# Redrawing the head of a fused linear-attention and squared-ReLU kernel: order of the first steps, place of one bias fetch, and the cut of the first weight block

## The chip, the cores and the metric

The kernel runs on one core of one Trainium2 chip. The metric is the device time of one execution in microseconds, lower is better. Where a profile is read, its times run from the start of the profiled span. Engines are named as the profile names them: PE (TensorE matmul), PEld (its weight load), DVE (VectorE), ACT (ScalarE), POOL (GpSimd) and SP (SyncE); SPq and ACTq are the queues on which SP and ACT issue DMAs.

## The reference, cut to what matters

```python
x = A_x                                   # 1 x 2048 x 448, bf16
xn = layernorm(x)                         # no scale, no shift, eps 1e-5
# A: linear attention, 16 heads of 28
q, k, v = split(xn @ wqkv)                # wqkv 448 x 1344
phi = lambda t: where(t > 0, t + 1, exp(t)) + 1e-6
kv = einsum("hsd,hse->hde", phi(k), v);  z = sum over s of phi(k)
s = (phi(q) @ kv / (phi(q) . z + 1e-6)) @ wo
# B: squared-ReLU block, 448 -> 1792 -> 448
h = relu(xn @ w1 + b1) ** 2
g = silu(h @ w2 + b2)
return x + s * g
```

## The kernel before, in words

The 2048 tokens are 16 tiles of 128 tokens, in 4 groups of 512. The 448 channels are 3 chunks of 128 and a rest of 64; matmuls on the rest use half of PE's rows, and the long streams pair two units on the two halves of the rows. The hidden width of 1792 is 14 chunks of 128.

A `Program` collects operations (`add`) with an engine, the tiles they read and write, and an assumed duration. PE and SP run in the order in which the program adds the operations: that order is written out by hand. The operations of ACT and DVE are ordered by a planner (`schedule`, `one_pass`) that walks through assumed times, assumed landing times of transfers among them; `behind` ties one operation behind another on its engine, `prio` puts it ahead. Every engine then runs its list strictly in order, waiting on semaphores. PSUM has 8 banks, which the planner hands out.

The **head** is what happens until the first long stream of matmuls. Its steps, by the labels used below:

- `load_x`, `load_main`, `load_rest`: DMAs. Tokens 0 and 1 one by one, 2 and 3 together; then k's weights (`wk`: chunks 0 to 2 on SP, the rest channels twice, one for each half of the rows, on ACT); then `w1` in blocks set by `cuts` (`w10`, `w11`, `w12`, `w13`, each with two rests), with the bias `b1r` behind `w10`. `late_loads` then queues the gates' bias `b2b`, the two halves of `w2` and q's weights `wq`.
- `bn`, `ag` (line 497, 498, DVE), `ln`, `rs` (505, 509, ACT), `xn` (527, DVE): layer norm of one tile. `tw` (543 on DVE, 544 on ACT) doubles the rest channels of a pair of tiles.
- `warm` (line 1223): matmuls on a zero tile that keep PE busy.
- `T0` to `T3` (`pe_transpose`, line 604): PE transposes the three full chunks of a tile; `eT` (613 on DVE, 614 on ACT) evicts them to `xT`. `TR0`, `TR2` (`pe_transpose_rests`, 628): the rests of a pair of tiles; `eTR` (638) evicts them.
- `K0.0`, `K1.0` (`k_part`, 803): k of tiles 0 and 1 on the full chunks; `Kr0` (`k_rests`, 818): their rest, with both `wk` rests. `phi` (709, 714, 721) turns them into phi(k).
- `Ha0.0`, `Ha1.0`, `Ha0.2`, `Ha1.2` (`head_part`, 831): hidden chunks 0 and 1 for tiles 0 and 1, then for tiles 2 and 3; `Hr0` (`head_rest`, 847): the rest. `B1`, `b1f` (`bias_cols`, 1238, 1241): transpose of `b1`, which every ReLU (line 766) needs.

Then follows the stream `H0.2` to `H0.13` (line 788): twelve hidden chunks of group 0, four at a time, then the second matmul (`G`, line 1094), k, q and so on, all in one order by hand.

Of the kernel before, what the change touches and what calls it, by code (L numbers as in the profile page):

```python
# [9 lines left out]
P = 128  # L10
S, D, F = 2048, 448, 1792
# [35 lines left out]
class Program:  # L47
# [6 lines left out]
    def add(self, eng, emit, reads=(), writes=(), dur=0.2, alts=(), nbytes=0, mode=None, label="", slow=1.0):  # L54
        op = Op(eng, emit, reads, writes, dur, alts, nbytes, mode, label)
        op.slow, op.behind, op.at = slow, None, None
        for t in op.reads:
            op.raw.add(self.writer[t])
            self.readers.setdefault(t, []).append(op)
        for t in op.writes:  # L60
            w = self.writer.get(t)
            if w is not None and w is not op:
                op.deps.add(w)
            for r in self.readers.get(t, ()):
                if r is not op:
                    op.deps.add(r)
            self.writer[t] = op
            self.readers[t] = [r for r in self.readers.get(t, ()) if r is op]
        op.raw.discard(op)
        op.deps |= op.raw  # L70
        for d in op.deps:
            d.succ.append(op)
        self.ops.append(op)
        return op
# [233 lines left out]
def bass_recurrent_scan__linear_attn_block__dense_activation_squared_relu__prompt_kernel(  # L308
    nc, A_x, A_wqkv, A_wo, B_x, B_w1, B_b1, B_w2, B_b2, out
):  # L310
    with ExitStack() as es:
# [3 lines left out]
        add = pr.add  # L315
# [4 lines left out]
        eps5 = sb("eps5", [P, 1], f32)  # L320
# [5 lines left out]
        x_tok = sb("x_tok", [P, NT, D], bf)  # L326
        xn = sb("xn", [P, NT, 512], bf)
        xT = sb("xT", [P, NT, 4, P], bf)
# [7 lines left out]
        b1r = sb("b1r", [NF, P], bf)  # L336
        b1f = sb("b1f", [P, NF], f32)
        b2b = sb("b2b", [P, D], bf)
        st6 = sb("st6", [P, NT, 6], f32)
# [26 lines left out]
        def ap(src, dims, offset=0):  # L366
            return bass.AP(tensor=src.tensor, offset=src.offset + offset, ap=dims)
# [59 lines left out]
        def dma(eng, dst, src, writes, nbytes, reads=(), dur=0.45, slow=1.0):  # L427
            return add(
                eng, lambda e, _: e.dma_start(dst, src), reads, writes, dur, nbytes=nbytes, label="dma" + str(writes[0]), slow=slow  # L429
            )  # L430
# [11 lines left out]
        def load_rest(eng, w, src, name, lo, hi, off=0, part=None):  # L442
            for i in (0, 1) if part is None else (part,):
                dma(
                    eng, w[64 * i : 64 * i + 64, 3, lo:hi], src[384:448, off + lo : off + hi], [(name, 3 + i)],
                    64 * (hi - lo) * 2, ["actw"] if eng == "act" else (), dur=0.58,
                )

        wn = lambda name: [(name, i) for i in range(5)]
        HA = 2  # L450
        cuts = (0, 4 * P, 6 * P, 10 * P, F)
        add("act", lambda e, _: e.preload_act_table_set("natural_log_exp_and_others"), [], ["actw"], 1.25, label="table").prio = -1e6
        load_x(0, 1, "sp")
        load_x(1, 2, "sp")
# [17 lines left out]
        late_constants()  # L472

        def late_loads():
            dma("sp", b2b[:, :], ap(B_b2, [[0, P], [1, D]]), ["b2b"], P * D * 2)
            for i, at in ((0, 17.9), (1, 20.8)):
                f0 = i * NF // 2
                dma(
                    "sp", w_2[:, f0 : f0 + NF // 2, :], B_w2[P * f0 : P * (f0 + NF // 2)].rearrange("(f p) d -> p f d", p=P),
                    [("w2", i)], F * D,  # L480
                ).at = at
            load_main("sp", w_q, A_wqkv, "wq", 0, D)
            load_rest("sp", w_q, A_wqkv, "wq", 0, D)

        def last_loads():
            load_x(12, 16)
# [6 lines left out]
        def hp(si, k):  # L493
            return None if si > 3 else 5 * si + k - 25

        def ln_stats(si):
            add("dve", lambda e, _: e.bn_stats(st6[:, si, :], x_tok[:, si, :]), [("x", si)], [("st", si)], 0.61, label=f"bn{si}").prio = hp(si, 0)  # L497
            add("dve", lambda e, _: e.bn_aggr(mv[:, si, :], st6[:, si, :]), [("st", si)], [("mv", si)], 0.16, label=f"ag{si}").prio = hp(si, 1) if si > 1 else si - 29

        def ln_rstd(lo, hi):  # L500
            c = slice(lo, hi)
            ts = range(lo, hi)
            add(
                "act",
                lambda e, _: e.activation(out=vep[:, c], in_=mv[:, c, 1], func=AF.Ln, bias=eps5[:, 0:1]),
                [("mv", i) for i in ts] + ["eps5", "actw"], [("vep", i) for i in ts], 0.3, label=f"ln{lo}",
            ).prio = -40 + lo if hi - lo == 1 else None
            add(
                "act", lambda e, _: e.activation(out=rstd[:, c], in_=vep[:, c], func=AF.Exp, scale=-0.5),  # L509
                [("vep", i) for i in ts], [("rstd", i) for i in ts], 0.2, label=f"rs{lo}",  # L510
            ).prio = -40 + lo if hi - lo == 1 else None

        def xn_cols(si, lo, hi):
# [20 lines left out]
        def ln_twin(lo, hi):  # L534
            ts = range(lo, hi)

            def twin(e, eng):
                dst, src = xn[:, lo:hi, 448:512], xn[:, lo:hi, 384:448]
                if lo >= 4 * SWAP:
                    both = xn[:, lo:hi, :].rearrange("p t f -> p (t f)")  # L540
                    dst, src = both[:, 896:1024], both[:, 768:896]
                if eng == "dve":
                    return e.tensor_copy(dst, src)
                return e.activation(out=dst, in_=src, func=AF.Copy)

            add("dve", twin, [("xn", i) for i in ts], [("xd", i) for i in ts], 0.18, alts=[("act", 0.27)], label=f"tw{lo}").prio = hp(lo + 1, 4)

        MM = lambda n: n / 2400 + 0.0025

# [69 lines left out]
                    0.15 + 0.07 * n if eng == "dve" else 0.18 + 0.107 * n, label=f"eT{si}.{lo}",  # L619
                ).prio = -30  # L620

        def pe_transpose_rests(lo):
            b = Buf("T")

            def f(e, _):
                v = ps(b)[:, :].bitcast(bf)
                for i in range(2):
                    last = e.transpose(v[:, i * P : (i + 1) * P], xn[:, lo + i, 384:512], ident[:, :])
                return last

            ts = (lo, lo + 1)
            add("pe", f, [("xd", i) for i in ts] + ["ident"], [b], 0.0558 * 2, mode="128", label=f"TR{lo}")

            def ev(e, eng):
                src = ps(b)[:, 0:P].bitcast(bf).rearrange("p (t k) -> p t k", t=2)
                if eng == "dve":
                    return e.tensor_copy(xT[:, lo : lo + 2, 3, :], src)
                return e.activation(out=xT[:, lo : lo + 2, 3, :], in_=src, func=AF.Copy)

            add("act", ev, [b], [("xT", i) for i in ts], 0.39, label=f"eTR{lo}").prio = -30  # L640

        def pe_transpose_two(lo):
            b = Buf("T")
# [573 lines left out]
        def warm(n, after=(), src=None):  # L1217
            b = Buf("W")

            def f(e, _):  # L1220
                last = None
                for _i in range(n):
                    last = e.matmul(ps(b)[:, 0:P], src or dum[:, 0:P], src or dum[:, 0:P], start=True, stop=True)
                return last

            add("pe", f, ["dum", *after] if src is None else [], [b], n * 0.107, mode="128", label="warm")
# [15 lines left out]

        warm(3, src=one)
        warm(30)
        warm(8, [("mv", 0)])
        pe_transpose(0, ((0, 3, "act"),))
        warm(3)
        pe_transpose(1, ((0, 3, "act"),))
        k_part(0, 0, 3)
        pe_transpose_rests(0)  # L1250
        k_part(1, 0, 3)
        head_part(0, 0)
        pe_transpose(2, ((0, 3, "act"),))
        head_part(0, 1)
        bias_cols()
        pe_transpose(3, ((0, 3, "dve"),))
        pe_transpose_rests(2)
        k_rests(0)
        head_part(2, 0)
        head_part(2, 1)  # L1260
        head_rest(0)

        byname = {op.label: op for op in pr.ops}
        for first, order in (
            (-26, "bn0 ag0 bn1 ag1 xn0 xn1 bn2 ag2 bn3 ag3 xn2 xn3"),
            (-61, "rs1 eT0.0 tw0 eT1.0 ln2 rs2 ln3 rs3 eTR0 eT2.0 b1f"),
        ):
            names = order.split()
            for i, (a, b) in enumerate(zip(names, names[1:])):
                byname[b].behind = byname[a]  # L1270
                byname[b].prio = first + 1 + i
            if first < -26:
                byname[names[0]].prio = first
        landing = {
            ("x", 0): 2.92, ("x", 1): 3.9, ("x", 2): 4.65, ("wk", 0): 5.7, ("wk", 3): 5.7, ("wk", 4): 7.2, ("w10", 0): 6.97,
            ("w10", 3): 7.2, ("w10", 4): 7.4, ("b1r", None): 7.5, ("w11", 0): 8.2, ("w11", 3): 8.4, ("w11", 4): 8.6,
            ("w12", 0): 9.7, ("w12", 3): 9.9, ("w12", 4): 10.1, ("x", 4): 11.3,
        }
        for (name, k), t in landing.items():
            byname["dma" + str((name, k) if k is not None else name)].at = t  # L1280
# [135 lines left out]
```

## Time and profile before

| | us |
|---|---|
| median of 3 runs | 143.53 (143.05 to 143.62) |
| profiled execution, its own time | 143.35 |
| its span | 142.1 |
| busy PE / DVE / ACT | 138.3 / 103.0 / 79.1 |
| first matmul of the stream `H0.2`.. | 10.82 after the start |
| last matmul but the tail's | about 138.3 |

The span leaves 1.25 us of the profiled execution's own time outside. In the rows of the timeline the first number is the start, the second the time from the first start to the last end of a merged row, and `x3` the number of instructions in it; ends of matmuls are modelled, so that the distance between starts, not the duration, gives the pace. A bracket tells how long the engine sat idle before the row and what released it.

### The profile page before, as it was taken

Reading aid. Unit: us, or ns where it says so; the run is one execution under the profiler, and the core shown is the slowest. Engines: PE = TensorE matmul, PEld = TensorE weight load, DVE = VectorE, ACT = ScalarE, POOL = GpSimd, SP = SyncE. Lnnn points to the kernel's source line nnn. Section 1 sums busy time; section 2 is a strip of 40 time slices with the busy share of each in tenths; the row PEclk is TensorE's granted clock in tenths of the full one; section 3 lists DMA queues with packets and bytes.
Section 4 is the critical chain, followed back from the end, with each engine's and each line's share of the span. In section 5 each row is a group of like instructions: output and inputs, shape, how many; then the busy total and the mean of one; then the engine's idle time right before and its main releaser. Section 6 shows DMA issues by size and latency. Waiting matters only on the chain.

```text
span 142.1 us, 3239 instructions
## 1 busy us (share of the span) xinstructions
PE 138.3 (97%) x1299; PEld 71.1 (50%) x1299; DVE 103.0 (72%) x222; ACT 79.1 (56%) x146; POOL 6.3 (4%) x40
## 2 busy tenths in 40 slices
PE   7999999999999999999999999999999999999992
PEld 7854445454444444444544444445547455555472
DVE  2848984899889897789777799786035516874875
ACT  3679797140888727697962757697139430301412
POOL 7900000000000000000000000000000000000000
PEclk9999999999999999999999999999999999999999
DMA  4998997349923000232000000000696000223033
GB/s 96 322 277 241 276 342 160 47 58 283 198 33 55 14 0 0 46 51 46 12 5 0 0 0 5 0 0 19 161 210 152 0 0 24 94 81 102 32 97 97
DMA packets 24220, 12.91 MB, mean 91 GB/s; under 512 B 14354, under 2 KB 23566, under 8 KB 24206
## 3 DMA queue, kind: packets, MB, share of 16 engines
q1 hardware_dynamic: 22414, 11.35, 31.8%
q10 hardware_dynamic: 1792, 1.36, 4.0%
q8 instruction: 10, 0.16, 0.5%
q14 instruction: 4, 0.03, 0.1%
HBM read 9.23 MB, written 1.90 MB: 78 GB/s over the span
## 4 chain that ended last, share of the span: by engine, by line
PE 91%; DMA 4%; DVE 2%; SPq 1%; issue 0%
PE pb L788 29%; PE pb L1094 22%; PE pb L1186 7%; PE pb L889 7%; PE pb L731 7%; PE pb L741 6%; PE pb L1111 4%; DMA w<-in_B_w_dram 4%; PE pb L1151 3%; PE pb L868 1%; SPq L429 1%; PE pb L831 1%; DVE gbuf L1175 1%; PE pb L895 1%; PE pb L1038 1%; PE pb L963 1%
## 5 line engine op out<-in xcount | busy, mean ns | idle before, releaser
L788 PE MATMUL pb<-xT,w 64*128 64x512 bf16 x378 | 43.6, 376 | 0.0
L1094 PE MATMUL pb<-w,r 64*128 64x448 bf16 x336 | 34.6, 349 | 0.0
L766 ACT ACTIVATE r<-pb,b1f 128x512 bf16<-128x512 f32 x40 | 25.7, 686 | 14.2 <-PE pb L788 13.8
L788 PEld LDWEIGHTS pb<-xT,w 64*128 64x128 bf16 x378 | 18.2, 94 | 21.8
L1094 PEld LDWEIGHTS pb<-w,r 64*128 64x128 bf16 x336 | 16.2, 94 | 16.0 <-issue 0.4
L778 ACT ACTIVATE r<-r 128x1024 bf16<-128x1024 bf16 x15 | 15.7, 1062 | 0.3
L763 DVE TENSOR_SCALAR r<-pb,b1f 128x512 bf16<-128x512 f32 x16 | 11.7, 744 | 3.2 <-PE pb L788 3.2
L1206 DVE TENSOR_TENSOR gbuf<-pb,gbuf 128x448 bf16<-128x448 f32 x14 | 8.1, 618 | 6.6 <-PE pb L1186 6.6
L497 DVE BATCH_NORM_STATS2 st<-x_tok 128x6 f32<-128x448 bf16 x16 | 9.6, 613 | 4.4 <-DMA x_tok<-in_A_x_dram 4.4
L731 PE MATMUL pb<-w_k,xT 64*128 64x448 bf16 x98 | 11.5, 349 | 0.0
L741 PE MATMUL pb<-xT,w_q 64*128 64x512 bf16 x84 | 11.0, 376 | 0.0
L1134 ACT ACTIVATE gbuf<-gbuf 128x448 bf16<-128x448 bf16 x14 | 7.0, 570 | 6.5 <-DVE gbuf L1084 5.9
L1186 PE MATMUL pb<-w_k,pqT 64*128 64x448 bf16 x96 | 10.5, 349 | 0.0
L1084 DVE TENSOR_TENSOR gbuf<-pb,b2b 128x448 bf16<-128x448 f32 x14 | 8.0, 614 | 3.4 <-PE pb L1094 2.0
L721 DVE SCALAR_TENSOR_TENSOR pk<-pb,pk 128x448 bf16<-128x448 f32 x16 | 9.6, 619 | 0.2
L889 PE MATMUL pb<-pk,xn 128*128 128x448 bf16 x48 | 9.6, 353 | 0.0
L709 ACT ACTIVATE pk<-pb 128x448 bf16<-128x448 f32 x16 | 7.8, 543 | 3.1 <-PE pb L731 2.5
L1002 DVE TENSOR_TENSOR pqT<-pqT,xT 128x2048 bf16<-128x2048 bf16 x3 | 3.7, 1222 | 8.0 <-DMA xT<-scr 8.0
L527 DVE TENSOR_SCALAR xn<-x_tok,mv,rstd 128x448 bf16<-128x448 bf16 x16 | 7.4, 499 | 1.6 <-ACT rstd L509 1.6
L777 DVE TENSOR_TENSOR r<-r 128x1024 bf16<-128x1024 bf16 x13 | 8.5, 682 | 0.1
L925 DVE TENSOR_TENSOR zacc<-zacc,pk 128x448 f32<-128x448 f32 x13 | 8.0, 617 | 0.1
L709 ACT ACTIVATE pqT<-pb 128x512 bf16<-128x512 f32 x12 | 6.5, 597 | 2.1 <-PE pb L741 2.1
(100 smaller groups left out, 134.1 us busy)
## 6 DMA issues: line engine op xcount, KB each, us to landing
w<-in_B_w_dram SPq DMA_DIRECT2D x2, 784.0 KB, 8.5
out_dram<-gbuf SPq DMA_DIRECT2D x14, 112.0 KB, 1.7
w<-in_B_w_dram SPq DMA_DIRECT2D x3, 384.0 KB, 4.9
xT<-gbuf SPq DMA_DIRECT2D x32, 32.0 KB, 2.0
x_tok<-in_A_x_dram SPq DMA_DIRECT2D x2, 448.0 KB, 5.7
x_tok<-in_A_x_dram SPq DMA_DIRECT2D x3, 224.0 KB, 3.1
xT<-scr SPq DMA_DIRECT2D x6, 112.0 KB
xT<-scr ACTq DMA_DIRECT2D x5, 112.0 KB
```

The source lines that it names most:

```text
L497: add("dve", lambda e, _: e.bn_stats(st6[:, si, :], x_tok[:, si, :]), [("x", si)], [("st", si)], 0.61, label=f"bn{si}").prio = hp(si, 0)
L709: "act", lambda e, _: e.activation(out=slot, in_=ps(buf)[0:rows, 0:n], func=AF.Exp), [buf, "actw"],
L721: lambda e, _: e.scalar_tensor_tensor(out=slot, in0=ps(buf)[0:rows, 0:n], scalar=1.0 + 1e-6, in1=slot, op0=ALU.add, op1=ALU.max),
L731: return e.matmul(ps(b)[:, 0:D], x_tile(rows, si, c), w_k[rows, c, :], start=start, stop=stop)
L741: return e.matmul(ps(b)[:, 0:512], w_q[rows, c, m * P : (m + 1) * P], x_group(rows, g, c), start=start, stop=stop,)
L763: return e.tensor_scalar(out=slot, in0=ps(b)[:, 0:512], scalar1=b1f[:, fi : fi + 1], scalar2=0.0, op0=ALU.add, op1=ALU.max)
L766: return e.activation(out=slot, in_=ps(b)[:, 0:512], func=AF.Relu, bias=b1f[:, fi : fi + 1])
L778: return e.activation(out=both, in_=both, func=AF.Square)
L788: return e.matmul(ps(b)[:, 0:512], w_1[rows, c, fi * P : (fi + 1) * P], x_group(rows, g, c), start=start, stop=stop,)
L889: last = e.matmul(ps(b)[:, 0:D], xn_cols(si, c * P, (c + 1) * P), pk[:, si, :], start=(si == 0), stop=(si == NT - 1),)
L1094: return e.matmul(ps(b)[:, 0:D], r_cols(rows, fi, si), w_2[rows, fi, :], start=start, stop=stop)
L1186: return e.matmul(ps(b)[:, 0:D], w, msb[rows, c, :], start=start, stop=stop)
```

## The change

Five things are done together.

1. `cuts`: the first block of `w1` has two hidden chunks instead of four, the second four instead of two. The number of DMAs stays.
2. `late_loads`: the DMA of `b2b` moves behind the three of `wq`; the planner is told 18.6 for the first half of `w2` instead of 17.9.
3. PE's order in the head is drawn up anew: 4 warm matmuls instead of 8 ahead of `T0`, 5 instead of 3 ahead of `T1`, 2 new ones ahead of `TR0`; `TR0` goes ahead of `K0.0`; `T2`, `Kr0` and `T3` go ahead of all `Ha`; `B1` goes behind `Ha1.2`.
4. `tw0`, `eTR0`, `eT2.0` and `eTR2` go from ACT to DVE, and the chains of DVE and ACT are written out anew. `bn2` goes ahead of `xn1`.
5. The planner's assumed durations of some layer-norm steps and its assumed landing times are others.

```diff
-        cuts = (0, 4 * P, 6 * P, 10 * P, F)
+        cuts = (0, 2 * P, 6 * P, 10 * P, F)
...
         def late_loads():
-            dma("sp", b2b[:, :], ap(B_b2, [[0, P], [1, D]]), ["b2b"], P * D * 2)
-            for i, at in ((0, 17.9), (1, 20.8)):
+            for i, at in ((0, 18.6), (1, 20.8)):
...
             load_main("sp", w_q, A_wqkv, "wq", 0, D)
             load_rest("sp", w_q, A_wqkv, "wq", 0, D)
+            dma("sp", b2b[:, :], ap(B_b2, [[0, P], [1, D]]), ["b2b"], P * D * 2)
...
-            add("act", ev, [b], [("xT", i) for i in ts], 0.39, label=f"eTR{lo}").prio = -30
+            add(eng, ev, [b], [("xT", i) for i in ts], 0.39 if eng == "act" else 0.25, label=f"eTR{lo}").prio = -30
...
         warm(3, src=one)
         warm(30)
-        warm(8, [("mv", 0)])
+        warm(4, [("mv", 0)])
         pe_transpose(0, ((0, 3, "act"),))
-        warm(3)
+        warm(5)
         pe_transpose(1, ((0, 3, "act"),))
+        warm(2)
+        pe_transpose_rests(0, "dve")
         k_part(0, 0, 3)
-        pe_transpose_rests(0)
         k_part(1, 0, 3)
+        pe_transpose(2, ((0, 3, "dve"),))
+        k_rests(0)
+        pe_transpose(3, ((0, 3, "dve"),))
         head_part(0, 0)
-        pe_transpose(2, ((0, 3, "act"),))
         head_part(0, 1)
-        bias_cols()
-        pe_transpose(3, ((0, 3, "dve"),))
-        pe_transpose_rests(2)
-        k_rests(0)
+        pe_transpose_rests(2, "dve")
         head_part(2, 0)
         head_part(2, 1)
+        bias_cols()
         head_rest(0)
...
-            (-26, "bn0 ag0 bn1 ag1 xn0 xn1 bn2 ag2 bn3 ag3 xn2 xn3"),
-            (-61, "rs1 eT0.0 tw0 eT1.0 ln2 rs2 ln3 rs3 eTR0 eT2.0 b1f"),
+            (-26, "bn0 ag0 bn1 ag1 xn0 bn2 xn1 ag2 tw0 bn3 ag3 eTR0 xn2 xn3 eT2.0 tw2 eT3.0 eTR2"),
+            (-61, "rs1 eT0.0 ln2 eT1.0 rs2 ln3 rs3 b1f"),
...
         landing = {
...
-            ("x", 0): 2.92, ("x", 1): 3.9, ("x", 2): 4.65, ("wk", 0): 5.7, ("wk", 3): 5.7, ("wk", 4): 7.2, ("w10", 0): 6.97,
+            ("x", 0): 2.8, ("x", 1): 3.45, ("x", 2): 4.45, ("wk", 0): 6.2, ("wk", 3): 6.1, ("wk", 4): 7.6, ("w10", 0): 7.25,
```

## The prediction, made before the changed kernel was run

> **What bounds the kernel now.** I read the page's busy times first, then the stretches around the point where the long stream of matmuls begins.
>
> ```profile
> PE 138.3 (97%) x1299; PEld 71.1 (50%) x1299; DVE 103.0 (72%) x222; ACT 79.1 (56%) x146; POOL 6.3 (4%) x40
> ```
>
> The table of stretches (PE busy is the first sum of each row) shows where PE's missing 3% lie.
>
> ```profile
> 0.00:6.43 6.43, 5.40 (x50) 5.28 (x51) 3.29 (x10) 2.98 (x8) 5.43 (x37) 1.00 0.70 199
> 6.43:10.82 4.39, 4.18 (x33) 2.35 (x35) 2.14 (x8) 3.31 (x11) 0.63 (x3) 1.00 1.04 276
> 10.82:138.34 127.52, 127.52 (x1206) 62.48 (x1203) 95.49 (x199) 72.04 (x126) 0.25 (x1) 1.00 0.33 79
> ```
>
> From 10.82 to 138.34 PE is never idle: DVE and ACT are free there for a quarter and more, and a DMA or a faster eviction can gain nothing as long as PE finds its data. Only what lies ahead of the first stream matmul at 10.82, and the 3.76 us of tail, can be won. The change touches the head alone. PE's rows in it:
>
> ```profile
> 5.17 0.53 PE L604 MATMUL pb<-ident,xn 128*128 128x128 bf16 x3
> 5.81 0.43 PE L604 MATMUL pb<-ident,xn 128*128 128x128 bf16 x3
> 6.43 0.73 PE L803 MATMUL pb<-w_k,xT 128*128 128x448 bf16 x3 [0.19 <-ACT xn L544]
> 7.11 0.73 PE L803 MATMUL pb<-w_k,xT 128*128 128x448 bf16 x3
> 8.00 0.50 PE L831 MATMUL pb<-xT,w 128*128 128x256 bf16 x3 [0.16 <-DMA w<-in_B_w_dram]
> 8.93 0.18 PE L1238 MATMUL pb<-ident,b1r 14*128 14x14 bf16 x1
> 9.22 0.28 PE L628 MATMUL pb<-ident,xn 128*128 128x128 bf16 x2
> 9.43 0.36 PE L818 MATMUL pb<-w_k,xT 64*128 64x448 bf16 x2
> 9.84 0.83 PE L831 MATMUL pb<-xT,w 128*128 128x256 bf16 x6
> 10.60 0.39 PE L847 MATMUL pb<-xT,w 64*128 64x512 bf16 x2
> 10.82 9.23 PE L788 MATMUL pb<-xT,w 64*128 64x512 bf16 x84
> ```
>
> Starts give the pace: `K0.0` at 6.43, `TR0` at 7.00, so 0.19 a matmul of 448 columns; the six `Ha` at 9.84 and `Hr0` at 10.60 give 0.11 each of 256 columns; three transposes take 0.17. So the gaps are: `K1.0` is through at 7.68 and `Ha0.0` starts at 8.00 (0.32, waits for `w10`); 0.09 ahead of `B1` (waits for `b1r`); 0.12 ahead of `Ha0.2` at 9.84, which waits for `eT3.0` (9.42 to 9.78). That is 0.53 of 4.39 us. Two DMAs of the head matter most (issued in the order seen here; last column: issue to landing):
>
> ```profile
> w_k<-in_A_wqkv_dram SPq DMA_DIRECT2D x1, 336.0 KB, 4.1
> w_k<-in_A_wqkv_dram ACTq DMA_DIRECT2D x1, 56.0 KB, 5.2
> w<-in_B_w_dram SPq DMA_DIRECT2D x1, 384.0 KB, 5.3
> ```
>
> `wk`'s chunks, issued at 2.18, land at 6.28; its second rest, issued at 2.7, at 7.9; `w10`, issued at 2.66, at 7.96.
>
> **The start of PE's useful work does not move.** `K0.0` needs `wk` (6.28, and 0.15 later it runs), whatever stands ahead of it. Four warm matmuls fewer let `T0` go when `xn0` is there (4.69): 4.78 instead of 5.17. `eT0.0` then runs 5.34 to 5.83. `bn2` (its tokens land at 4.4) now goes ahead of `xn1`: 4.63 plus 0.53, the pace of `bn4` and `bn5`, so `xn1` runs 5.16 to 5.56 instead of 5.01 to 5.41. Five warm matmuls at 0.107 end at 5.63; `T1` starts at 5.65, still ahead of 5.81. `eT1.0` ends at about 6.66 (6.80 before), in time for `K1.0` at 7.00. `tw0` on DVE: 5.6 to 5.8; two warm matmuls; `TR0` at 6.17 to 6.28, while PE has to wait for `wk` anyway. So `TR0` goes out of the way of `K1.0` and costs nothing; if `wk` landed before 6.1 it would cost its 0.11.
>
> **The chain for tiles 2 and 3.** `ag3` ends at 6.5. `eTR0` on DVE stands ahead of `xn2`. No row shows it there: between 0.20 (the 128x128 copy) and 0.36 (128x384 out of PSUM), I take 0.28, as its 256 columns are nearer to the second. It runs 6.5 to 6.8 and frees `xn2` at the very moment when `rs2` ends (ACT: `ln2` 5.73, `eT1.0` 6.17, `rs2` 6.54 to 6.75); at 0.36 `xn2` is 0.08 later, without effect. `xn2` 6.8 to 7.2, `xn3` 7.2 to 7.6: PE asks for them at 7.57 and 8.1.
>
> **The new order on PE** from 6.43: `K0.0` and `K1.0` 1.14, `T2` 0.17, `Kr0` 0.19, `T3` 0.17, four `Ha` 1.31, `TR2` 0.11, `B1` 0.11 (8.93 to 9.04), `Hr0` 0.22 (10.60 to 10.82), and three changes between whole and half rows at 0.10 (from `TR2` at 9.22 to `Kr0` at 9.43 are 0.21, two transposes are 0.11): 0.30. Sum 3.72, so the stream would start at 10.15 instead of 10.82: **0.67 earlier**. Cross-check: 4.39 less 0.53 of gaps, less 0.11 for `TR0`, leaves 3.75.
>
> Each wait in that order: `Kr0` at 7.83 needs the second `wk` rest (7.9 before; it shares the DMA engines with a `w10` that is 192 KB smaller). At the 293 GB/s of 5 to 8 us that is up to 0.67 us earlier, and no earlier at the least; at 7.9 and 0.05 of waking `Kr0` loses 0.13. I take nothing lost, since both landed together at 7.9 and half of one is gone. `Ha0.0` at 8.28 needs `w10`, at worst 7.96: no gap either way. `Ha0.2` at 9.05 needs `eT3.0`: `T3` 8.12 to 8.45, eviction to 8.85. `Hr0` at 9.93 needs `eTR2`: `TR2` is out at 9.2, eviction to 9.5, and `phi` of `Kr0` shares DVE then: a 0.62 long step (line 721) in front puts it at 10.0, and `Hr0` 0.1 to 0.15 late. So the head is worth between 0.4 and 0.67; below that would take a landing beyond what the rows show.
>
> **What lies behind the head** now has to be there 0.67 earlier. `w11` in all is as many bytes as before up to its end: 9.4 against 10.15. `w12`'s last rest: 12.5 against 13.2. `w13`'s: 15.4 against 16.2. The first half of `w2`: 19.3 against 20.65 less 0.67, and 112 KB of `b2b` now come behind it (0.4 at 280 GB/s, a gain in slack). `wq`: 23.5 against 24.5. `b2b` itself lands near 23.6 and is first used by line 1084 at 34.2. Behind it on SP's queue stand tokens 8 to 11, which lose nothing in order, and the transposes' copies, which end near 27 for a use at 33.3. So the moved fetch is worth nothing by itself; if all that slack were gone it would cost its 0.4. The evictions moved from ACT to DVE lie in the stretch in which DVE was idle for half of its time.
>
> **Two rules of the skill.** The second rest of `wk` comes on ACT's queue, and its 56 KB took 5.2 us beside SP's. The Trainium skill, DMA: Bandwidth & Descriptors, Queues, rings and completion order, says that each engine takes turns between the queues packet by packet; by that rule a smaller block on SP's queue would not speed ACT's up, `Kr0` would wait to 7.96, and the gain would be 0.54. No row here separates the two.
>
> The warm matmuls start 0.107 apart and `T1`'s are the last at that pace; `T2`'s are 0.056 apart, though the granted clock reads 1.00 in every stretch. The Trainium skill, TensorE: Matmul & The Clock Gate, Part 1, says that a free-running window of 3.4 us must be busy before the full rate comes; its Part 4 says that transposes don't count as busy. It would speak against shifting warm matmuls about; the rival below prices this from rows.
>
> **The rivals.**
> - *A wait stays in the head* (`Kr0` on the rest of `wk`, or `eTR2` behind `phi`): gain 0.4 to 0.55, 142.8 to 143.0. For it: the 7.9 of the row, and that DVE's order decides. Chance 0.12.
> - *Given back later.* Every order on DVE and ACT is drawn anew by the planner from other times. The tightest place in the rows is around 94 us: `zsb` ends at 94.48 and PE needs it at 94.82, with 0.69 long steps of line 721 beside it on DVE. One such step in front costs 0.35, two of them 1.0, and a bank held back in each of two or three groups of the stream 0.7 apiece: 143.0 to 144.6. Against it: before has no such wait in 127 us. Chance 0.12, half of it up to 143.8.
> - *PE stays slow longer* (slower than before). Place: the transition that here comes at about 6.05. Idle slivers of 0.03 to 0.05 appear ahead of `T0` and `T1`. If the full pace came later by d, PE would do its 3.72 at half pace for d: d/2 lost. From d = 1.3 the gain is gone; from d = 3.2 the time is over 144.25, slower by what can be told; if all of the head runs at half pace it is 3.7 more, 146.4. With one window of the Trainium skill's page as d, 3.4, it would be 144.4. Against it: 44 warm matmuls and six transposes ahead of `K0.0` in both kernels, and slivers of a few hundredths. Chance 0.05, with another 0.05 for a stall of this size that no row announces.
> - *Nothing changes on the path*: were `K1.0` late because `xn1` is, or `xn2` behind `eTR0`, the head would start as before, 143.4. Slack is 0.3 at both. Chance 0.04.
>
> **How the numbers follow.** The profiled execution took 143.35, 0.18 under the median. 143.35 less 0.67 is 142.68. I do not add the 0.18: the landing of `w10` at 7.96, which PE waited for, differs between executions, and now has 0.3 of slack. So 142.7, chance 0.62, its own range 142.45 to 142.9. The range reaches to the lesser half of the give-back: 142.4 to 143.8. A measurement of this kernel can tell about 0.5%, 0.72 us: faster is below 142.81, slower above 144.25. Of the forecast's 0.62, 0.57 lie below the first bound: faster 0.57. Same: its other 0.05, the wait left in the head 0.12, half of the give-back 0.06, nothing changed 0.04: 0.27. Slower: the other half of the give-back 0.06, the slow pace 0.05, the unannounced stall 0.05: 0.16.
>
> **What the profile would show.** Right: the first row of line 788 starts near 10.15; `K0.0` still at 6.4; `TR0` (628) ahead of it; no gap ahead of line 831; `Kr0` at 7.8 to 8.0; no PE wait behind the head. Wrong: a gap ahead of line 818 of over 0.2, line 847 waiting for DVE, matmuls 0.37 apart after 6.5, or PE idle between 10 and 138.

## The result, and the profile after

The changed kernel takes 142.88 us in the median of 9 runs (142.37 to 143.16), the kernel before 143.51 (143.05 to 143.64): a ratio of 0.9955, 95% interval 0.9939 to 0.9971. By the medians that is 0.63 us less; by the ratio 0.45%. The profiled execution took 142.37, the fastest of the nine, with a span of 141.1.

The page's busy times and the table of stretches, cut at `K0.0` and at the first stream matmul:

```profile
PE 137.6 (97%) x1299; PEld 70.9 (50%) x1299; DVE 104.0 (74%) x226; ACT 77.4 (55%) x142; POOL 6.3 (4%) x40
```

```profile
6.15:9.87 3.72, 3.72 (x34) 2.35 (x33) 3.27 (x12) 2.14 (x7) 0.91 (x4) 1.00 0.90 252
9.87:138.00 128.13, 128.13 (x1213) 63.41 (x1210) 95.98 (x200) 71.54 (x128) 0.24 (x1) 1.00 0.34 83
```

From 6.15 to 9.87 PE is busy for all of 3.72 us; before, the stretch that did this work (with `TR0` inside) was 4.39 long and held 0.53 of gaps. DVE is busy for 3.27 of 3.72 where it was 2.14 of 4.39, and does not hold PE up. PE's rows in the timeline:

```profile
4.86 0.40 PE L604 MATMUL pb<-ident,xn 128*128 128x128 bf16 x3
5.09 0.44 PE L1223 MATMUL pb<-dum 128*128 128x128 bf16 x5
5.74 0.34 PE L604 MATMUL pb<-ident,xn 128*128 128x128 bf16 x3 [0.20 <-DVE xn L527]
...
6.03 0.28 PE L628 MATMUL pb<-ident,xn 128*128 128x128 bf16 x2
6.15 1.30 PE L803 MATMUL pb<-w_k,xT 128*128 128x448 bf16 x6
7.28 0.33 PE L604 MATMUL pb<-ident,xn 128*128 128x128 bf16 x3
7.54 0.36 PE L818 MATMUL pb<-w_k,xT 64*128 64x448 bf16 x2
...
8.02 0.82 PE L831 MATMUL pb<-xT,w 128*128 128x256 bf16 x6
...
9.65 0.39 PE L847 MATMUL pb<-xT,w 64*128 64x512 bf16 x2
```

No row from `K0.0` on carries a bracket: nothing is waited for any more. The stream starts at 9.87 instead of 10.82. `K0.0` itself runs at 6.15 instead of 6.43: in this execution `wk` was there at 6.05, and PE came to its full pace at about 5.0 (five warm matmuls in 0.44), not at 6.05. So 0.28 of the 0.95 by which the stream starts sooner here is luck of this execution, and 0.67 is the shorter head. This profile therefore shows more gain than the median.

From the stream's start to the last matmul, before and after are alike to a few hundredths. The profiled execution's time less the stream's start is 132.53 before (143.35 less 10.82) and 132.50 after (142.37 less 9.87). This difference is the yardstick below: **132.5 where PE never waits behind the head; what is over is time given back.**

### The profile page after: what moved, and what is told of

It is laid out like the page before. It is cut to its first block, busy times and chain, and to the rows that moved or that the text cites. A ratio compares the mean times of both kernels' runs of the same rounds, so it can differ in the third digit from the quotient of the medians.

```text
span 141.1 us, 3239 instructions
## 1 busy us (share of the span) xinstructions
PE 137.6 (97%) x1299; PEld 70.9 (50%) x1299; DVE 104.0 (74%) x226; ACT 77.4 (55%) x142; POOL 6.3 (4%) x40
## 4 chain that ended last, share of the span: by engine, by line
PE 93%; DVE 3%; DMA 1%; issue 0%
PE pb L788 29%; PE pb L1094 23%; PE pb L1186 8%; PE pb L889 7%; PE pb L731 7%; PE pb L741 6%; PE pb L1111 4%; PE pb L1151 3%; DMA x_tok<-in_A_x_dram 1%; PE pb L868 1%; DVE st L497 1%; DVE gbuf L1175 1%; PE pb L895 1%; PE pb L831 1%; PE pb L1038 1%; PE pb L803 1%
## 5 line engine op out<-in xcount | busy, mean ns | idle before, releaser
L766 ACT ACTIVATE r<-pb,b1f 128x512 bf16<-128x512 f32 x39 | 25.2, 686 | 12.3 <-PE pb L788 12.0
L763 DVE TENSOR_SCALAR r<-pb,b1f 128x512 bf16<-128x512 f32 x17 | 12.4, 745 | 4.1 <-PE pb L788 3.9
L721 DVE SCALAR_TENSOR_TENSOR pqT<-pb,pqT 128x512 bf16<-128x512 f32 x12 | 7.7, 682 | 0.0
```

The lines of the kernel that those rows point to most:

```text
L721: lambda e, _: e.scalar_tensor_tensor(out=slot, in0=ps(buf)[0:rows, 0:n], scalar=1.0 + 1e-6, in1=slot, op0=ALU.add, op1=ALU.max),
L763: return e.tensor_scalar(out=slot, in0=ps(b)[:, 0:512], scalar1=b1f[:, fi : fi + 1], scalar2=0.0, op0=ALU.add, op1=ALU.max)
L766: return e.activation(out=slot, in_=ps(b)[:, 0:512], func=AF.Relu, bias=b1f[:, fi : fi + 1])
```

## The experiments

**One part at a time.** Theory: PE's new order carries the gain, the other parts nothing by themselves. Rivals: the cut is what gains; the moved fetch is a part of it; the planner's redrawn orders give or take.

The cut alone, on the kernel before:

```diff
-        cuts = (0, 4 * P, 6 * P, 10 * P, F)
+        cuts = (0, 2 * P, 6 * P, 10 * P, F)
```

> The kernel before with the new cut of w1 alone (two chunks in the first block, four in the second); order, chains, b2b and the planner's tables as before. Theory (the order carries most of the gain): w10 lands near 7.1 instead of 7.96 and b1r near 7.8 instead of 8.9, so the gaps of 0.32 ahead of the first line 831 and of 0.09 ahead of B1 close; the wait for eT3.0 stays; the stream starts near 10.45 instead of 10.82: 143.1 to 143.2, 0.3 to 0.4 faster than before. Rival (the cut is what gains, the order only comes along): the stream starts near 10.2, 0.6 faster. Rival (tiles 2 and 3 set the head's end): the gaps move to T2 and T3, no gain.

Measured: 143.45, ratio 1.0000 (0.9983 to 1.0017). Nothing is gained: the theory's time was wrong. Its account of the head was not: from `K0.0` to the stream it is 4.06 here, against 4.39 before and the 4.02 that the theory comes to. The stream starts at 9.95 instead of the forecast 10.45 because `wk` landed early in this execution, at 5.76. The profile, of an execution of 142.98, shows where time is given back; PE and DVE in the timeline:

```profile
5.89 0.73 PE L803 MATMUL pb<-w_k,xT 128*128 128x448 bf16 x3
...
9.95 3.19 PE L788 MATMUL pb<-xT,w 64*128 64x512 bf16 x28
13.47 0.82 PE L788 MATMUL pb<-xT,w 64*128 64x512 bf16 x6 [0.32 <-ACT rstd L509]
```

```profile
9.85 0.62 DVE L721 SCALAR_TENSOR_TENSOR pk<-pb,pk 128x448 bf16<-128x448 f32 x1
11.36 1.15 DVE L497 BATCH_NORM_STATS2 st<-x_tok 128x6 f32<-128x448 bf16 x2 [0.89 <-DMA x_tok<-in_A_x_dram]
...
12.65 0.24 DVE L714 TENSOR_SCALAR pk<-pk 128x448 bf16<-128x448 bf16 x1
12.92 0.62 DVE L721 SCALAR_TENSOR_TENSOR pk<-pb,pk 128x448 bf16<-128x448 f32 x1
```

The second group of four chunks, wanted 3.02 after the first at 12.97, starts at 13.47: 0.5 given back (142.98 less 9.95 is 133.03). The bracket names ACT's `rs4`, but by the kernel this matmul does not depend on `rs4`. It depends on the first group's first ReLU and on phi of `K0`, both over by 10.9, and on `w12`, whose second rest, issued at 8.33, landed at 13.27:

```profile
w<-in_B_w_dram SPq DMA_DIRECT2D x1, 64.0 KB, 4.9
```

So `w12`'s landing held it. DVE meanwhile stood 0.89 idle at the head of its list, waiting for tokens 4 and 5, with phi of `K1` queued behind; phi of `K1` ended at 13.54, and the next unit of the stream, which needs it, would have run at 13.83 (0.86 after 12.97) without the gap. That wait cost nothing here.

The new order with the old cut:

```diff
-        cuts = (0, 2 * P, 6 * P, 10 * P, F)
+        cuts = (0, 4 * P, 6 * P, 10 * P, F)
```

> The changed kernel with the old cut of w1 (four chunks in the first block). Theory: the order alone keeps most of the gain. w10 lands near 7.96 and is needed at 8.0 to 8.3; the second rest of wk lands near 7.9 and now holds Kr0 until 7.95, with T3 and all Ha behind it, 0.1 to 0.4 later than in the changed kernel: the stream starts between 10.1 and 10.3, 142.9 to 143.1. Rival (ACT's queue takes its turns whatever SP's block is, so the second rest of wk lands as in the changed kernel, near 7.2): no wait at Kr0, the stream within 0.1 of the changed kernel's. Rival (the cut is what gains): 143.3 or more.

Measured: 142.83 (142.51 to 143.06), ratio 0.9964 (0.9950 to 0.9979); stream at 10.03 in an execution of 142.52, no wait behind the head.

```profile
6.28 1.30 PE L803 MATMUL pb<-w_k,xT 128*128 128x448 bf16 x6
...
10.03 9.23 PE L788 MATMUL pb<-xT,w 64*128 64x512 bf16 x84
```

The order keeps the gain without the cut, all of it and not only most, as the first rival had it: the second rest of `wk` landed at 7.35 here and held nothing.

The moved fetch undone in the changed kernel:

```diff
         def late_loads():
+            dma("sp", b2b[:, :], ap(B_b2, [[0, P], [1, D]]), ["b2b"], P * D * 2)
...
             load_rest("sp", w_q, A_wqkv, "wq", 0, D)
-            dma("sp", b2b[:, :], ap(B_b2, [[0, P], [1, D]]), ["b2b"], P * D * 2)
```

> The changed kernel with b2b fetched ahead of w2, as before. Theory: w2's halves land some 0.4 later, with 0.7 and more of slack left, so PE waits nowhere and the time is that of the changed kernel within 0.15. Rival (the moved fetch is part of the gain): PE waits ahead of the first line 1094 and the time is 0.3 to 0.4 over the changed kernel's.

Measured: 142.76, ratio 0.9961 (0.9946 to 0.9975), no PE wait behind the head: the fetch is worth nothing here.

The planner's tables alone, on the kernel before (the new assumed durations and landing times, and the 18.6). The line that lets `tw0` choose ACT stays as it was, so that nothing in the edit holds `tw0` on DVE; the planner put it there by itself.

```diff
...
-            ("x", 0): 2.92, ("x", 1): 3.9, ("x", 2): 4.65, ("wk", 0): 5.7, ("wk", 3): 5.7, ("wk", 4): 7.2, ("w10", 0): 6.97,
+            ("x", 0): 2.8, ("x", 1): 3.45, ("x", 2): 4.45, ("wk", 0): 6.2, ("wk", 3): 6.1, ("wk", 4): 7.6, ("w10", 0): 7.25,
...
```

> The kernel before with the planner's new assumed durations, landing times and the 18.6 alone (tw0 held on DVE as these lines have it); order of PE, chains, cut and b2b as before. Theory: the planner draws other orders on DVE and ACT, but PE waits no longer anywhere: 143.5, within 0.2 of before. tw0 on DVE between xn1 and bn2 or later moves the head by 0.1 at most. Rival (the redrawn orders are a part of the gain or take some of it): 0.3 or more off in either direction, with PE waits behind 11 us.

Measured: 143.45, ratio 0.9999 (0.9986 to 1.0012); stream at 10.82 as before, no wait behind it. So the cut and the tables alone move nothing, and without the moved fetch nothing is lost; what is left is the new order on PE with its chains on DVE and ACT.

**Which part of the order.** PE's order stays new; `tw0`, `eTR0`, `eT2.0` and `eTR2` go back to ACT:

```diff
...
-            (-26, "bn0 ag0 bn1 ag1 xn0 bn2 xn1 ag2 tw0 bn3 ag3 eTR0 xn2 xn3 eT2.0 tw2 eT3.0 eTR2"),
-            (-61, "rs1 eT0.0 ln2 eT1.0 rs2 ln3 rs3 b1f"),
+            (-26, "bn0 ag0 bn1 ag1 xn0 bn2 xn1 ag2 bn3 ag3 xn2 xn3 tw2 eT3.0"),
+            (-61, "rs1 eT0.0 tw0 ln2 eT1.0 rs2 ln3 rs3 eTR0 eT2.0 eTR2 b1f"),
```

> The changed kernel with PE's new order, but tw0, eTR0, eT2.0 and eTR2 left on ACT as before the change. tw0 then ends at 6.0 (TR0 wants it at 6.1), eTR0 near 7.5 (Kr0 wants it at 7.6 to 7.8), eT2.0 at 8.1, eTR2 behind the two exponentials of phi near 9.4 (Hr0 wants it at 9.65 to 9.9). Theory (PE's order carries the gain, the engines of the evictions little): within 0.2 of the changed kernel, 142.8 to 143.1. Rival (ACT is too full in the head, which is why they were moved): Kr0 waits for eTR0 or Hr0 for eTR2, 0.3 or more over the changed kernel.

Measured: 142.97 (142.51 to 143.04), ratio 0.9957 (0.9943 to 0.9971). The stream started at 9.79 in its profile, so the head ran as fast as with the evictions on DVE; ACT had room. PE's order is what gains: from `K0.0` to the stream it is 3.72 to 3.75 in all six profiles of the new order in which no row of the head waits for a landing (the changed kernel, old cut, bias first, this one, and the two with three chunks further down), against 4.39 before. No run has PE's new order alone on the kernel before, so a share of `bn2` ahead of `xn1` or of the tables together with the order is not excluded. But this execution took 142.96, 133.17 over its start, and PE shows where:

```profile
9.79 1.46 PE L788 MATMUL pb<-xT,w 64*128 64x512 bf16 x12
...
13.33 1.04 PE L788 MATMUL pb<-xT,w 64*128 64x512 bf16 x8 [0.35 <-DMA w<-in_B_w_dram]
```

The second group waits for `w12` (issued at 8.37, 4.9 to landing), 0.52 after it is wanted; by the starts the third waits another 0.13 for `w13`, whose last rest landed at 16.45, too short a wait for a bracket.

**What gives the cut's gain back.** Theory A: DVE's and ACT's old orders, with phi of `K1` behind tokens that come late. Theory B: `w12`'s landing. The cut alone, with the layer norm of tiles 4 and 5 held behind phi of `K1`:

```diff
-        for a, b in [('bn6', 'sq0.2.3'), ('bn7', 'bn6')]:
+        for a, b in [('bn6', 'sq0.2.3'), ('bn7', 'bn6'), ('bn4', 'maK1'), ('bn5', 'bn4')]:
```

> The cut alone, with one thing more: the layer norm of tiles 4 and 5 is held behind the last phi step of K1 on DVE. In the cut alone the stream started at 9.95, and 0.49 was lost at the second group of four chunks; there DVE had waited 0.89 for tokens 4 and 5 (landed 11.3) with phi of K1 behind it, ACT had ln4 ahead of the second group's ReLUs, and w12's last rest landed at 13.27. Theory A (the old order on DVE and ACT, made for the old head, gives the cut's gain back behind late tokens): the gap goes or shrinks under 0.2, 142.9 to 143.15. Theory B (w12's landing does it): gap and time as in the cut alone, 143.4.

Measured: 143.13 (142.74 to 143.47), ratio 0.9978 (0.9967 to 0.9989). Phi of `K1` now ends at 11.76 instead of 13.54, and no gap follows:

```profile
11.14 0.62 DVE L721 SCALAR_TENSOR_TENSOR pk<-pb,pk 128x448 bf16<-128x448 f32 x1
11.68 1.14 DVE L497 BATCH_NORM_STATS2 st<-x_tok 128x6 f32<-128x448 bf16 x2
```

The time is what theory A said, and by itself it would speak for A. The profiles speak for B: in the cut alone `w12` held PE and phi of `K1` did not, and in this execution `w12` landed at 12.83, ahead of its use at 13.43 (the stream started at 10.40). The intervals of the two kernels overlap by a little. So B is shown in one execution of the cut alone, and what holding the layer norm back is worth (143.13 against 143.45) stays open. The kernels above and below show B again; A's mechanism shows in one of them, the one with the half rows together.

**The price of the slow pace.** The changed kernel without warm matmuls:

```diff
-        warm(3, src=one)
-        warm(30)
-        warm(4, [("mv", 0)])
...
-        warm(5)
...
-        warm(2)
```

> The changed kernel without any warm matmul. Theory (PE's pace follows the work it has had): PE's first work is T0 at 4.8, so the full pace comes several us later than in the changed kernel, where it came at 4.9 after 4 us of warm matmuls; the transposes and K0.0 to about 8.5 or 9 run at half pace (448 columns 0.37 apart), 1.2 to 1.8 lost: 144.0 to 144.7. Rival (the pace comes by itself at a fixed moment after the start): within 0.2 of the changed kernel.

Measured: 144.81, ratio 1.0096 (1.0077 to 1.0114), 1.9 more than the changed kernel; a little over my range.

```profile
5.16 0.50 PE L604 MATMUL pb<-ident,xn 128*128 128x128 bf16 x3 [5.16 <-DVE xn L527]
...
6.54 2.45 PE L803 MATMUL pb<-w_k,xT 128*128 128x448 bf16 x6
...
10.02 1.49 PE L831 MATMUL pb<-xT,w 128*128 128x256 bf16 x6
11.30 0.36 PE L628 MATMUL pb<-ident,xn 128*128 128x128 bf16 x2
11.50 0.82 PE L831 MATMUL pb<-xT,w 128*128 128x256 bf16 x6
...
12.58 1.68 PE L788 MATMUL pb<-xT,w 64*128 64x512 bf16 x14
```

The same six matmuls take 1.49 at 10.02 and 0.82 at 11.50. From `K0.0` to the stream it is 6.04 instead of 3.72, 2.32 more; the prediction's d/2, with d from 6.54 to 11.3, gives 2.38. The rival's price was right, its condition did not come.

**Attempts to go further.** With the head dense, I tried to shorten it and to bring the weights sooner.

`Kr0` next to `Hr0`, so that PE changes between whole and half rows once instead of three times:

```diff
         pe_transpose(2, ((0, 3, "dve"),))
-        k_rests(0)
-        pe_transpose(3, ((0, 3, "dve"),))
         head_part(0, 0)
+        pe_transpose(3, ((0, 3, "dve"),))
         head_part(0, 1)
         pe_transpose_rests(2, "dve")
+        bias_cols()
         head_part(2, 0)
         head_part(2, 1)
-        bias_cols()
+        k_rests(0)
         head_rest(0)
```

> The changed kernel with Kr0 put directly ahead of Hr0 (both on half rows), B1 ahead of Ha0.2, T3 behind Ha0.0: two of the three changes between whole and half rows fall away, 0.10 each, and up to 0.06 comes back as a wait of Ha0.2 for eT3.0. Theory (PE's own work sets the head from K0.0 on): the stream starts 0.15 earlier, 142.65 to 142.75. Rival (the landing of w1's later blocks is now the bound): no gain in time, and a gap shows in line 788 at the second or third group of four chunks, or ahead of the first.

Measured: 144.14, ratio 1.0038 (1.0021 to 1.0056), slower than before the change. `Hr0` ran at 9.46, 0.19 sooner (0.10 of it because `K0.0` ran at 6.05), but then:

```profile
10.22 3.20 PE L788 MATMUL pb<-xT,w 64*128 64x512 bf16 x28 [0.38 <-DMA w<-in_B_w_dram]
13.79 1.04 PE L788 MATMUL pb<-xT,w 64*128 64x512 bf16 x8 [0.38 <-DVE r L763]
15.55 0.82 PE L788 MATMUL pb<-xT,w 64*128 64x512 bf16 x6 [0.72 <-ACT r L766]
```

```profile
11.71 1.15 DVE L497 BATCH_NORM_STATS2 st<-x_tok 128x6 f32<-128x448 bf16 x2 [2.92 <-DMA x_tok<-in_A_x_dram]
...
15.85 0.27 DVE L714 TENSOR_SCALAR pk<-pk 128x448 bf16<-128x448 bf16 x1
```

The stream waits for `w11`'s second rest, as the rival had it. Then two gaps follow in the second group, which wait for evictions on DVE and ACT and not for a landing, as neither theory had it: with `Kr0` late the planner put the statistics of tiles 4 and 5 first; DVE waited 2.92 for those tokens, and evictions and phi (15.85) stood behind.

Tokens 6 and 7 behind `w13`, and the planner's landing times to match:

```diff
-            if i == 2:
+            if i == 3:
                 load_x(6, 8, "sp")
...
```

> The changed kernel with tokens 6 and 7 fetched behind w13 instead of ahead of it, and the planner's landing times to match. In the changed kernel w13's last rest lands at 15.75 and the third group of four chunks asks for it at 15.91; its runs spread over 0.8. Theory (some executions stall there): w13 lands 0.5 to 0.7 earlier, median 142.5 to 142.65 and the highest run below 143. Rival (the spread comes from the start of the head, tokens, wk or PE's pace): median and spread as in the changed kernel.

Measured: 142.91 (142.47 to 143.60), ratio 0.9972 (0.9958 to 0.9987): no gain, no smaller spread. Two of `w13`'s three loads landed sooner (14.70 and 15.03 instead of 15.30 and 15.57), but the last one later (16.17 instead of 15.75), so the run did not bring what the theory asked for. A wait for `w13` shows only in the run with the evictions on ACT (0.13); that it makes the spread is not shown. Here the profile shows a wait elsewhere, at the first group, although `Hr0` was through:

```profile
9.63 0.39 PE L847 MATMUL pb<-xT,w 64*128 64x512 bf16 x2
10.23 1.47 PE L788 MATMUL pb<-xT,w 64*128 64x512 bf16 x12 [0.22 <-DMA w<-in_B_w_dram]
```

The second rest of `w11` took 4.1 from its issue at 6.1. With the new cut the stream's first unit needs `w11`; with the old one it needs `w10` alone, and `w11` 0.86 later.

Three chunks in either block; the same without the two warm matmuls ahead of `TR0`; and the old cut without them:

```diff
-        cuts = (0, 2 * P, 6 * P, 10 * P, F)
+        cuts = (0, 3 * P, 6 * P, 10 * P, F)
...
-        warm(2)
```

> The changed kernel with three chunks in w1's first block and three in the second. So far the order with the old cut was as fast as with the new one; with the new cut the second rest of w11 landed between 9.6 and 10.2 in seven profiles and once held the stream's start (0.22), with the old cut between 9.2 and 9.4, but w10 at 7.8 to 8.0, just ahead of its use. Theory: both blocks have slack, the stream starts dense behind K0.0: 142.6 to 142.8 with a smaller spread. Rival (neither landing matters in most executions): 142.85, as the changed kernel.

Measured: 142.90 (142.39 to 143.76), ratio 0.9971 (0.9953 to 0.9989). The rival was right. In the profiled execution (142.67) all landings had slack and the stream started at 10.15.

> The same with the two warm matmuls ahead of TR0 left out. They take 0.11 at full pace and 0.21 at half pace between T1 and TR0, and in three of four profiles of the new order wk had landed by 6.05 and K0.0 followed TR0 at once. Theory (T1, TR0, K0.0 is then the chain): K0.0 and the stream start 0.1 to 0.2 earlier, 142.5 to 142.7. Rival (wk's landing or w11's bounds it, or the pace of PE comes later without them): no gain or 0.1 slower.

Measured: 142.89 (142.37 to 143.45), ratio 0.9955 (0.9936 to 0.9973). No gain, as the rival had it. `K0.0` came at 6.04 and the stream at 9.76, earlier than in any other profile, yet this execution took 143.45:

```profile
13.97 0.39 PE L788 MATMUL pb<-xT,w 64*128 64x512 bf16 x2 [1.03 <-DMA w<-in_B_w_dram]
```

1.2 us of the second group went into waiting for `w12`, whose second rest took 5.6 from its issue at 8.37.

> The new order with the old cut and without the two warm matmuls ahead of TR0. Ha0.0 is then wanted near 7.95 to 8.05 and w10 lands at 7.8 to 8.0. Theory: 0.1 earlier than with them, 142.7; w10 takes the rest of what they cost. Rival: w10's landing holds Ha0.0 and nothing is gained, 142.85.

Measured: 142.84 (142.54 to 143.21), ratio 0.9956 (0.9940 to 0.9971), as the rival said, but by another wait, the one that the prediction had priced for `Kr0`. PE's row, and the DMA issued at 2.73 with its time to landing:

```profile
8.09 0.36 PE L818 MATMUL pb<-w_k,xT 64*128 64x448 bf16 x2 [0.44 <-DMA w_k<-in_A_wqkv_dram]
```

```profile
w_k<-in_A_wqkv_dram ACTq DMA_DIRECT2D x1, 56.0 KB, 5.3
```

None of these beats the changed kernel. The order with the old cut equals it, with a narrower spread (0.55 in ten runs, 0.79 in nine).

## Why the prediction was right, and where it was not

- **Time and range.** 142.7 was forecast, 142.88 came; the range held it. Of the three outcomes I had put 0.57 on more than 0.5% faster; 0.45% came, so it was the second outcome by a little, and the interval lies on both sides of the bound.
- **The step that was off** is the last of "How the numbers follow": I did not add the 0.18 by which the profiled execution was under the median, since the wait for `w10` would now have slack. Median to median the gain is 0.63, next to the 0.67 of the sum; with the 0.18 the forecast would have been 142.86. One landing did leave the path, but the spread grew from 0.59 to 0.79 instead of shrinking. In the profiles of the new order with its warm matmuls two things vary: when `K0.0` starts (0.46) and what is given back behind the head (up to 0.65, and 1.4 with the half rows together). Which of them lifts the changed kernel's own median over 142.7 is not shown, since its one profile is its fastest execution. That 142.88 lies just inside the forecast's own range of 142.45 to 142.9 owes something to luck.
- **The new order on PE.** The sum of 3.72 was met to the hundredth (6.15 to 9.87). `eTR0` took 0.26 where 0.28 was taken; `xn2` started at 6.81 where 6.8 was said.
- **`K0.0` does not move.** Wrong for the profiled execution (6.15). With `wk` landed at 6.05 and PE at full pace early, the chain was `xn1`, `T1`, two warm matmuls, `TR0`: the case of an early `wk` that I had named and priced at 0.11. (In the profile before, `K0.0`'s bracket names ACT's `tw0`, on which it does not depend; `wk`, as I read it, landed at 6.30.) Over the profiles of the new order with its warm matmuls it runs at 6.05 to 6.51.
- **`Kr0` and the second rest of `wk`.** Rightly put at "nothing lost" with the new cut: it landed at 7.18. The Trainium skill's rule (DMA: Bandwidth & Descriptors, Queues, rings and completion order), as I drew it out, would have left it at 7.9. The runs go against what I drew from it: behind the 384 KB block it landed between 7.35 and 8.05 in four profiles, behind 192 or 288 KB between 6.74 and 7.30 in ten. They do not go against the rule itself. The new cut also halves the rows of that block from 1024 to 512 bytes, and between 5 and 6 us a packet took 46 ns (median) in the profile before and 27 ns in the changed kernel's, so that turns packet by packet would come round sooner too. No run separates the two.
- **`eTR2` behind phi** did not come: DVE waited 0.18 for `TR2` and evicted from 8.99 to 9.28, ahead of `Hr0` at 9.65.
- **What lies behind the head.** Right for `b2b`, `w2` and `wq`: no PE wait in the changed kernel, nor with `b2b` first. Mis-sized for w1: "9.4 against 10.15" for `w11` rested on equal bytes, and it landed at 9.65, in the other profiles with the new cut at 9.5 to 10.2 (9.2 to 9.4 with the old). For `w12`, 12.5 was taken; the profiles show 11.8 to 13.9.
- **The rivals.** "Given back later" has a real mechanism, but not at 94 us: at the second group of the stream, by `w12`'s landing, or, with the half rows together, by tokens 4 and 5 with evictions queued behind them. The slow pace, forced, costs what was said.

What stays open: why with the new cut `w11`'s last rest and the tokens behind it land later, although as many bytes were queued ahead. Tokens 4 and 5 landed at 9.6 to 9.8 in four profiles with the old cut and at 10.2 to 11.9 in eight with the new one.

## What to carry to other kernels

Where one engine is busy without a gap from some point on, only the start of that stretch counts: add up the work ahead of it, compare with the span, and the gaps are all there is to win. Removing one wait moves the whole stream against the next landings, so list what each later group needs, by when, and how far that landing varies between profiles, before a further tenth is sought. A bracket names the last report on a counter that the step waits on; before a cause is built on it, read from the kernel what the step needs, as the cut alone shows. And an engine that works strictly in order should not have a step that waits for a late transfer ahead of one that frees a bank (1.4 us behind the stream's start in the run with the half rows together).

## What the runs showed of the hardware

- PE's full pace came at different times in executions whose first matmuls were the same: the starts of warm matmuls and transposes go from 0.107 to 0.056 apart at 3.8 with the bias first, at about 5.0 in the changed kernel's profile and near 6.2 with only the cut changed back, while the granted clock reads 1.00 throughout. This agrees with the free-running window of the Trainium skill, TensorE: Matmul & The Clock Gate, Part 1. But 3.8 is only 2.9 behind the first matmul at 0.84, less than the 3.4 of a busy window that this part of the Trainium skill gives; there the measurement decides. The pace is one of the things that move `K0.0`, and not the only one: it started at 6.15 in the changed kernel's profile and at 6.28 with only the cut changed back, but at 6.51 with the bias first, where token 1 landed at 4.01 instead of 3.26.
- A step between whole-row and half-row matmuls costs PE 0.10 us: the changed kernel's last transpose of `T2` and `Kr0` start 0.15 apart, where transposes start 0.056 apart.
